# A delta-rule attention and two expert layers on one core: copies moved to DMA, squares to ScalarE, and a shorter inversion of the first four tiles

## Chip, cores and metric

The kernel runs on one core of one Trainium2 chip. The metric is the device time of one execution, in microseconds (us). Lower is better. The kernel before takes 950.15 us (median of 3 runs, 949.26 to 957.06).

## What is computed

An attention with a delta-rule state feeds a mixture-of-experts layer, and that feeds a second one. The change touches the attention alone:

```python
k_n = k / (np.linalg.norm(k, axis=-1, keepdims=True) + 1e-06)
for t in range(S):                      # B=4, H=8, S=768, D=48
    y[:, :, t] = einsum('bhd,bhde->bhe', q[:, :, t], state)
    v_old = einsum('bhde,bhd->bhe', state, k_n[:, :, t])
    state += beta[:, :, t] * outer(k_n[:, :, t], v[:, :, t] - v_old)
x = y as rows of tokens (3072 x 384)
x = moe(x, ...)     # each token to the expert with the largest logit
x = moe2(x, ...)    # each expert takes N/E tokens, largest logits first
```

## The kernel before

**Tiles.** The tokens are 24 tiles of 128, six to a batch. A tile holds 8 heads and two chunks of 64 tokens, so 16 blocks of 64x64. Inside a chunk the recurrence over tokens becomes a triangular solve: with A the strictly triangular matrix of products of keys, scaled by beta, the inverse of I + A is applied to keys and values (`solve`), and only then does the state pass from chunk to chunk (`chain`).

**One tile's preparation.** `a_trans` (L202) transposes keys and queries on TensorE (PE), `a_copy` (L216) brings them to the tile KQ on ScalarE (ACT), `a_gram` (L224) multiplies them, and `a_mask` (L234) scales by beta and masks, into the tile AT. The mask is done on VectorE (DVE) by line L243, or split: ACT scales (L241) and GpSimd (POOL) multiplies with the mask (L247). `a_diag` (L249) copies the 32x32 blocks on the diagonal to Dc, on ACT (L263), POOL (L261) or DVE (L259), as the tables `DP` and `DIA` say. `kbeta` (L196) and `vscale` (L189) are multiplications on POOL. Norms: `norm_sq` squares keys (L156 on POOL, but L153 and L154 on DVE and ACT for the first four tiles), `norm_sum` and `norm_fin` add and invert on DVE, with a root on ACT between them (L168).

**The inversion.** `stage_b` (L265) inverts the 32x32 blocks of four tiles at once on DVE: a transposition (L269), 30 steps of a multiplication (L280) and an addition (L284), and two transpositions out (L288, L290). It is a generator: `bs(k)` takes k pieces of it. Group 0 (tiles 0 to 3) is inverted before the loop starts, group g during the four tiles before its use; the tables `NB0`, `NB1`, `MB` and `PB` say how many pieces go where. `place` (L293) copies the inverted blocks into XT, half on ACT (L300) and half on POOL (L298), and `join1`, `join2` (L303, L317) make the off-diagonal 32x32 block of each 64x64 inverse by small matmuls on PE (L312, L324) with copies on ACT (L315, L327).

**The loop.** `go` (L406) first prepares eight tiles, then runs over n = 0 to 24. Iteration n does `solve(n)` (L339: 8 matmuls with 128x128 weights), `zcopy` on ACT (L343), `prod` (L353), `psub` on DVE (L357), then `chain(n)` in two halves (L379), while it prepares tile n+8, pieces of a stage are taken on DVE, and XT is filled for tile n+1. There is one XT, so `place(n+1)` comes after `solve(n)`. Each engine takes its instructions in the written order. The SyncE queue (SP) issues nearly all DMAs: the token loads of `load_tok` (two per tile), `store` of a tile (L399) and, in iterations 2, 5, 8 and 11, sixteen loads of keys and values for three tiles (L138).

**After the loop** the expert layers run; the change leaves them as they are.

```python
            if n % 4 == 0 and g < NG:          # L513, in the loop
                self.b = self.stage_b(g)
            bs(nb)
            if 0 < n < NT:
                for c in range(2):
                    self.solve(n, c)
                    self.zcopy(c)
```

Of the kernel before, what the change touches and what calls it, by code (L numbers as in the profile page):

```python
# [28 lines left out]
WM = (30, 2, 3)  # L29
HB = 60  # L30
# [5 lines left out]
class Attention:  # L36
    def __init__(self, tc, ctx, q, k, v, beta, w_gate, bias_t, consts, xbuf, LG):
# [14 lines left out]
        self.KQ = c1.tile([128, SLOTS, 4, 2, 128], F32, name="KQ")  # L52
# [10 lines left out]
        self.Dc, self.XTc, self.XN, self.R = {}, {}, {}, {}  # L63
# [8 lines left out]
        early = [self.w.tile([128, 32, 32], F32, name=x, bufs=1).rearrange("p u i -> p (u i)").rearrange("p (a h d) -> p a h d", a=2, h=8)  # L72
                 for x in ("XTc", "XN")]
# [72 lines left out]
    def norm_sq(self, n, cnt=3):  # L146
# [102 lines left out]
    def a_diag(self, n, pool=True):  # L249
# [4 lines left out]
        for qd in range(4):  # L254
# [10 lines left out]
    def stage_b(self, g):  # L265
# [5 lines left out]
        yield  # L271
        nc.vector.memset(X.rearrange("p i j -> p (i j)")[:, 0:1024:33], 1.0)
        for j in range(1, 31):
            m = 31 - j

            h = (17 if j < 11 else 24 if j < 19 else 28 if j < 25 else 30) - j - 1
            parts = [(0, h), (h, m)] if g == 0 and min(h, m - h) * j >= HB else [(0, m)]
            t = tmp[:, :m * j].rearrange("p (i c) -> p i c", c=j)
            for i, k in parts:
                nc.vector.tensor_mul(t[:, i:k], X[:, j + 1 + i:j + 1 + k, j:j + 1].to_broadcast([128, k - i, j]),  # L280
                                     X[:, j:j + 1, :j].to_broadcast([128, k - i, j]))
            yield
# [1553 lines left out]
```

## Time and profile before

| what | value |
| --- | --- |
| median of 3 runs | 950.15 us (949.26 to 957.06) |
| the profiled execution | 951.86 us |
| its span, first to last instruction | 950.1 us |
| mean granted TensorE clock | 0.944 of 2.4 GHz |
| PE, weight loads, DVE, ACT, POOL busy | 834.7, 746.8, 657.3, 454.1, 335.5 us |

The profile is one execution recorded by the hardware. Times in it count from its first instruction; 1.76 us of the execution lie outside of the span. A row of a timeline has the start, the duration, the engine, the line, what is written and read, the shapes, the number of merged instructions, and in brackets the idle time of the engine ahead of it with what ended it. A row of windows has the stretch, its length, the busy time of each engine with the number of instructions, the granted TensorE clock, the DMA share and GB/s.

### The profile page before, as it was taken

How to read it: one execution, taken by the hardware profiler on the slowest of the kernel's cores; microseconds unless marked ns; L12 is line 12 of the kernel's file. 1: busy time of each engine (PE TensorE's matmuls, PEld its weight loads, DVE VectorE, ACT ScalarE, POOL GpSimd, SP SyncE). 2: the span in 40 equal slices, each digit the busy share in tenths (PEclk: the TensorE clock that was granted, in tenths of full speed). 3: DMA queues.
4: the chain of work that ended last, by engine and by line, in shares of the span. 5: the costliest groups of instructions: out<-in, count | busy, mean ns of one | idle time of the engine just before them, and what ended most of it. 6: DMA issues, size and time to landing. Idle time of an engine off the chain costs nothing. (4 is left out here: it accounts for less than half of the span.)

```text
span 950.1 us, 22994 instructions
## 1 busy us (share of the span) xinstructions
PE 834.7 (88%) x9024; PEld 746.8 (79%) x9031; DVE 657.3 (69%) x1744; ACT 454.1 (48%) x990; POOL 335.5 (35%) x504
## 2 busy tenths in 40 slices
PE   5559879897888996999999999988899999897996
PEld 4458768786777885699989999864778888796996
DVE  4997989989797966665744555226877867776531
ACT  3556676585757676445445544220343243233431
POOL 7255444444443122521132221122353444343411
PEclk9877897897979799999999999999999999999999
DMA  9661152342500004563185431402244235324600
GB/s 155 112 107 27 37 101 56 81 80 57 111 11 19 28 28 161 169 221 126 37 284 172 152 107 35 154 29 83 78 170 165 80 123 176 119 66 167 201 26 29
DMA packets 141319, 98.28 MB, mean 103 GB/s; under 512 B 102757, under 2 KB 123268, under 8 KB 141204
## 3 DMA queue, kind: packets, MB, share of 16 engines
q1 hardware_dynamic: 134484, 76.67, 30.0%
q0 software_dynamic: 6720, 20.07, 6.7%
q8 instruction: 74, 1.21, 0.5%
q14 instruction: 41, 0.34, 0.1%
HBM read 82.36 MB, written 14.55 MB: 102 GB/s over the span
## 5 line engine op out<-in xcount | busy, mean ns | idle before, releaser
L1079 PE MATMUL ph<-xT,HL 128*128 128x384 f32 x1152 | 232.4, 345 | 11.2 <-DVE hh L1087 9.4
L1099 PE MATMUL po<-HL,hh 128*128 128x384 f32 x1152 | 238.3, 345 | 0.2 <-DVE hh L1087 0.2
L1079 PEld LDWEIGHTS ph<-xT,HL 128*128 128x128 f32 x1152 | 202.2, 190 | 21.4 <-DVE hh L1087 11.7
L1099 PEld LDWEIGHTS po<-HL,hh 128*128 128x128 f32 x1152 | 196.9, 189 | 3.6 <-issue 0.7
L1082 ACT ACTIVATE hh<-ph 128x384 fp32r<-128x384 f32 x128 | 62.7, 491 | 180.1 <-PE ph L1079 167.2
L1050 DVE TENSOR_TENSOR HL<-raw,HL 128x768 fp32r<-128x768 f32 x104 | 105.4, 1023 | 57.8 <-ACT HL L1049 57.4
L1087 DVE SCALAR_TENSOR_TENSOR hh<-ph,hh 128x384 fp32r<-128x384 f32 x128 | 70.6, 552 | 80.2 <-ACT hh L1082 80.1
L1049 ACT ACTIVATE HL<-raw 128x768 fp32r<-128x768 f32 x128 | 103.4, 839 | 33.7 <-DMA raw<-in_moe_w_dram 33.7
L280 DVE TENSOR_TENSOR Dtmp<-Dt 128x30 f32<-128x30 f32 (+22 forms) x199 | 89.2, 456 | 3.9
L379 PE MATMUL pc<-SI,R 112*48 112x56 f32 (+1 forms) x1536 | 65.2, 239 | 20.8 <-DVE R L357 16.5
L284 DVE TENSOR_TENSOR Dt<-Dt,Dtmp 128x30 f32<-128x30 f32 (+22 forms) x199 | 80.4, 412 | 3.0
L379 PEld LDWEIGHTS pc<-SI,R 112*48 112x48 f32 (+1 forms) x1536 | 57.4, 148 | 28.9 <-DVE R L357 19.8
L357 DVE TENSOR_TENSOR R<-pz,C 112x448 f32<-112x448 f32 x96 | 57.2, 614 | 19.5 <-ACT lgr L387 10.8
L1050 POOL TENSOR_TENSOR HL<-raw,HL 128x768 fp32r<-128x768 f32 x24 | 46.4, 1942 | 64.3 <-ACT HL L1049 64.2
L1137 POOL DMA_INDIRECT x2buf<-x,pidx x24 | 23.8, 990 | 106.1 <-ACT x L1133 86.1
L339 PE MATMUL pz<-RK,XT 128*128 128x96 f32 x384 | 60.4, 323 | 0.0
L353 PE MATMUL pz<-AT,Z 64*112 64x112 f32 x768 | 52.6, 279 | 7.4 <-ACT Z L343 7.3
L232 PE MATMUL pa<-KQ 64*64 64x128 f32 x640 | 49.0, 302 | 10.3 <-ACT KQ L221 10.2
L339 PEld LDWEIGHTS pz<-RK,XT 128*128 128x128 f32 x384 | 56.1, 232 | 1.6
L353 PEld LDWEIGHTS pz<-AT,Z 64*112 64x112 f32 x768 | 44.0, 184 | 12.5 <-ACT Z L343 9.2
L232 PEld LDWEIGHTS pa<-KQ 64*64 64x64 f32 x640 | 40.0, 150 | 14.1 <-ACT KQ L221 11.3
L1605 POOL DMA_INDIRECT out_dram<-x,oid x24 | 25.6, 1066 | 55.9 <-ACT x L1602 46.1
(408 smaller groups left out, 1257.3 us busy)
## 6 DMA issues: line engine op xcount, KB each, us to landing
raw<-in_moe_w_dram SPq DMA_DIRECT2D x68, 768.0 KB, 6.8
xbuf<-xt SPq DMA_DIRECT2D x24, 196.0 KB, 2.0
qt<-in_q_dram SPq DMA_DIRECT2D x22, 192.0 KB, 3.9
kt<-in_k_dram SPq DMA_DIRECT2D x21, 192.0 KB, 3.6
RK<-in_k_dram SPq DMA_DIRECT2D x48, 72.0 KB, 2.8
RK<-in_v_dram SPq DMA_DIRECT2D x48, 72.0 KB, 2.7
RK<-in_k_dram SPq DMA_DIRECT2D x8, 96.0 KB, 4.5
RK<-in_v_dram SPq DMA_DIRECT2D x8, 96.0 KB, 3.1
```

The lines of the kernel that those rows point to most:

```text
L232: nc.tensor.matmul(pg[r, p], KQ[:, 0:64], KQ, start=True, stop=True)
L280: nc.vector.tensor_mul(t[:, i:k], X[:, j + 1 + i:j + 1 + k, j:j + 1].to_broadcast([128, k - i, j]), X[:, j:j + 1, :j].to_broadcast([128, k ...
L284: nc.vector.tensor_add(X[:, j + 1 + i:j + 1 + k, :j], X[:, j + 1 + i:j + 1 + k, :j], t[:, i:k])
L339: nc.tensor.matmul(pz[:, p], self.XT[0][:, u], self.RK[:, n % RSLOTS, u], start=True, stop=True)
L353: nc.tensor.matmul(self.pr[h][:, p], self.Z[r, u], self.AT[r, n % SLOTS, u, 64:176], start=True, stop=True)
L379: nc.tensor.matmul(self.pc[r, hd], self.Rb[n % 2][0:112, hd % 2, c, hd // 2, r], SI[0:112, hd], start=True, stop=True)
L1049: nc.scalar.activation(t[:, i, 0, c], self.raw[s][i][:, c], AF.Copy)
L1050: (nc.gpsimd if pool else nc.vector).tensor_sub(t[:, i, 1, c], self.raw[s][i][:, c], t[:, i, 0, c].bitcast(F32))
L1079: nc.tensor.matmul(self.ph, W[:, i, a, c], x[:, k, b], start=(k == 0 and n == 0), stop=(k == 2 and n == 2))
L1082: nc.scalar.activation(h[:, 0], self.ph, AF.Relu)
L1087: self.nc.vector.scalar_tensor_tensor(h[:, 1], ph, 0.0, h[:, 0].bitcast(F32), op0=OP.max, op1=OP.subtract)
L1099: nc.tensor.matmul(self.po[s][t], h[:, a, r], W[:, 2 + i, b, c], start=(f == 0 and n == 0), stop=(f == 7 and n == 2))
```

## The change

Five things are changed, all in the attention.

1. Squares of keys (`norm_sq`) go from POOL to ACT for all tiles after the first four.
2. In the loop, `a_diag` of three tiles in four goes from POOL to four DMAs on SP (table value 3), and `place` of tiles 2 to 23 goes from ACT and POOL to four DMAs on SP.
3. `solve` takes each 128x128 matmul as two of 64x64, on the halves of the partitions.
4. For group 0, `stage_b` is rewritten: it inverts 16x16 blocks (14 steps, both blocks of a 32x32 block in one instruction). `join0a` and `join0b` then make the 32x32 inverses of one tile: 32 and 48 matmuls of 32x32, one subtraction and three scaled additions on DVE. The old way is kept as `stage_c` for the groups 1 to 5. Both inverses now lie in one tile, XTN, with two buffers.
5. The preparation is reordered: `go` writes out the first tiles, tiles 4 to 7 are masked whole on DVE, `stage_b(0)` runs in one piece before their masks, and the products, masks and diagonals of tiles 6 and 7 go into iterations 0 and 1. `stage_c(1)` starts in iteration 1 (before: 0) and is paced by new tables NF0, NF1. The idle matmuls of `warm` are no longer called. KQ keeps two slots of keys and eight of queries.

```diff
-NB0, NB1 = (7, 8, 8, 30), (3, 6, 0, 3)
+NB0, NB1, NF0, NF1 = (7, 8, 8, 30), (3, 6, 0, 3), (0, 12, 12, 30), (0, 8, 6, 0)
-SPL, DIA, QO = (0, 0, 1, 0), (0, 1, 1, 1), (0, 1, 1, 1)
+SPL, DIA, QO = (0, 0, 1, 0), (0, 3, 3, 3), (0, 1, 1, 1)
...
 def norm_sq
-            nc.gpsimd.tensor_mul(sq, K, K)
+            nc.scalar.activation(sq, K, AF.Square)
...
 def a_diag
+            elif pool == 3:
+                nc.sync.dma_start(o, i)
...
 def stage_b
+        def blocks(i, j, rows, cols):
+            x = X[:, i:i + 1, j:j + 1]
+            n, m = rows[0], cols[0]
+            return bass.AP(tensor=x.tensor, offset=x.offset, ap=[x.ap[0], [528, 2], [rows[1], n], [cols[1], m]])
+        nc.vector.memset(X[:, 16:32, 0:16], 0.0)
+        nc.vector.memset(X.rearrange("p i j -> p (i j)")[:, 0:1024:33], 1.0)
+        for j in range(1, 15):
+            m = 15 - j
+            t = tmp[:, :2 * m * j].rearrange("p (b i c) -> p b i c", b=2, c=j)
+            nc.vector.tensor_mul(t, blocks(j + 1, j, (m, 32), (j, 0)), blocks(j, 0, (m, 0), (j, 1)))
+            yield
+            r = blocks(j + 1, 0, (m, 32), (j, 1))
+            nc.vector.tensor_add(r, r, t)
+            yield
+        yield from self.turn(g, X)
...
+    def join0a(self, n):
...
+        for u in range(8):
+            for qd in range(4):
+                r, i0 = slice(32 * qd, 32 * qd + 32), 32 * (qd % 2)
+                nc.tensor.matmul(pt[r, u], self.AT[r, sl, u, i0:i0 + 32], D[r, u], start=True, stop=True)
+        nc.vector.tensor_sub(t0, pt, D)
+    def join0b(self, n):
...
+        for u in range(8):
+            for qd in range(4):
+                r = slice(32 * qd, 32 * qd + 32)
+                nc.tensor.matmul(px[r, 0, u], t0[r, u], DT[r, u], start=True, stop=True)
+        for u in range(8):
+            for qd in (0, 2):
+                r = slice(32 * qd, 32 * qd + 32)
+                nc.tensor.matmul(px[r, 1, u], DT[r, u], t0[r, u], start=True, stop=True)
+        for qd in (0, 2):
+            r = slice(32 * qd, 32 * qd + 32)
+            nc.vector.scalar_tensor_tensor(D[r], D[r], 2.0, px[r, 1], op0=OP.mult, op1=OP.add)
+        nc.vector.scalar_tensor_tensor(DT, DT, 2.0, px[:, 0], op0=OP.mult, op1=OP.add)
...
 def place
-            if qd % 2:
-                self.nc.gpsimd.tensor_copy(self.XT[0][r, :, r], self.XTc[n // 4][r, us])
+            if n > 1:
+                self.nc.sync.dma_start(self.XT[0][r, :, r], self.of(n, 0)[r])
...
 def solve
-            nc.tensor.matmul(pz[:, p], self.XT[0][:, u], self.RK[:, n % RSLOTS, u], start=True, stop=True)
+            for h in range(2):
+                r = slice(64 * h, 64 * h + 64)
+                nc.tensor.matmul(pz[r, p], self.XT[0][r, u, r], self.RK[r, n % RSLOTS, u], start=True, stop=True)
...
 def go
+        self.join0a(0)
+        self.join0b(0)
+        self.norm_sum(6, 3)
+        self.norm_root()
+        self.place(0)
+        self.vscale(0, 1)
+        self.join1(0)
+        self.join0a(1)
+        masks(4)
+        self.join2(0)
+        self.join0b(1)
+        self.vscale(1, 3)
+        masks(5)
+        self.norm_fin(6, 3)
...
             if n == 0:
                 for c in range(2):
                     self.solve(n, c)
                     self.zcopy(c)
+                self.join0a(2)
+                gram(6)
+                self.join0b(2)
+                masks(6)
...
```

On DVE, the kernel before has this from the last pieces of group 0's stage to the first of group 1's (L288 and L290 transpose group 0 out, L269 transposes group 1 in, and its steps begin):

```order
L288 STREAM_TRANSPOSE XN<-Dt 128x32x32
L290 STREAM_TRANSPOSE XTc<-Dt 128x32x32
L269 STREAM_TRANSPOSE Dt<-Dc 128x1024
L272 MEMSET Dt 128x32
L280 TENSOR_TENSOR Dtmp<-Dt 128x30
L284 TENSOR_TENSOR Dt<-Dt,Dtmp 128x30
L280 TENSOR_TENSOR Dtmp<-Dt 128x58
L284 TENSOR_TENSOR Dt<-Dt,Dtmp 128x29x2
```

The changed kernel has this ahead of group 1's first transposition (L297), in iterations 0 and 1: L334 is the subtraction of `join0a`, L350 and L351 are the additions of `join0b`, L418 is `psub(0)`, and the masks L243 are those of tile 6, then of half of tile 8 and of tile 7:

```order
L334 TENSOR_TENSOR t_816<-pm,XTN 128x256
L350 SCALAR_TENSOR_TENSOR XTN<-XTN,pm 32x256 x2
L351 SCALAR_TENSOR_TENSOR XTN<-XTN,pm 128x256
L243 SCALAR_TENSOR_TENSOR AT<-pa,bp,mask 128x128 x8
L418 TENSOR_TENSOR R_95<-pz,C_92 112x448 x4
L334 TENSOR_TENSOR t_1049<-pm,XTN 128x256
L350 SCALAR_TENSOR_TENSOR XTN<-XTN,pm 32x256 x2
L351 SCALAR_TENSOR_TENSOR XTN<-XTN,pm 128x256
L243 SCALAR_TENSOR_TENSOR AT<-pa,bp,mask 128x128 x12
L297 STREAM_TRANSPOSE Dt<-Dc 128x1024
```

The joins of tiles 2 and 3, twenty mask instructions and `psub(0)` now stand ahead of that transposition, and the joins of tiles 0 and 1 with the masks of tiles 4 and 5 stand ahead of these.

On SP the kernel before has, from the end of iteration 5 to that of iteration 6 (the sixteen loads, tile 16's tokens, the store of tile 5):

```order
L138 DMA RK<-in_k_dram 64x6x48 x8
L138 DMA RK<-in_v_dram 64x6x48 x8
L127 DMA kt_87<-in_k_dram 128x8x48
L127 DMA qt_89<-in_q_dram 128x8x48
L399 DMA xbuf<-xt 128x392
```

and the changed kernel, in the same place:

```order
L138 DMA RK<-in_k_dram 64x6x48 x8
L138 DMA RK<-in_v_dram 64x6x48 x8
L261 DMA Dc<-AT 32x8x32 x4
L127 DMA kt_87<-in_k_dram 128x8x48
L127 DMA qt_89<-in_q_dram 128x8x48
L357 DMA XT_91<-XTN 32x8x32 x4
L460 DMA xbuf<-xt 128x392
```

The copies of `a_diag` (L261) and of `place` (L357) now stand in SP's order behind the sixteen loads, the second of them ahead of the next tile's `solve`.

On PE, the changed kernel has between the last transposition before the loop and the first `solve` (L400): L333 is `join0a`, L343 and L347 `join0b`, L372 `join1`, L383 `join2`:

```order
L333 MATMUL pm<-XTN,AT 32x32 x32
L343 MATMUL pm<-XTN,t_546 32x32 x32
L347 MATMUL pm<-t_546,XTN 32x32 x16
L372 MATMUL pm<-XTN,AT 32x32 x16
L333 MATMUL pm<-XTN,AT 32x32 x32
L383 MATMUL pm<-XTN,t_641 32x32 x16
L343 MATMUL pm<-XTN,t_661 32x32 x32
L347 MATMUL pm<-t_661,XTN 32x32 x16
L400 MATMUL pz<-RK,XT_91 64x96 x16
```

All of these write the one buffer of `pm`, each after its reader on DVE or ACT is done; before, only `join1`, `join2` and the idle matmuls stood there.

## Rows read from the trace of the kernel before

**Rows 1.** All-engine windows: the inversion of group 0, then iterations 4 to 15.

```profile
31.00:78.00 47.00, 25.49 (x286) 23.33 (x287) 46.03 (x126) 20.75 (x63) 20.47 (x18) 0.75 0.55 98
130.00:297.60 167.60, 144.21 (x2594) 127.88 (x2592) 148.72 (x336) 112.86 (x291) 73.24 (x108) 0.88 0.32 66
```

**Rows 2.** DVE timeline, from the first masks to iteration 9.

```profile
22.36 1.13 DVE L243 SCALAR_TENSOR_TENSOR AT<-pm,bp,mask 128x128 f32<-128x128 f32 x4 [1.21 <-PE pm L232]
...
33.75 2.09 DVE L284 TENSOR_TENSOR Dt<-Dt,Dtmp 128x30 f32<-128x30 f32 x1
...
44.68 1.33 DVE L165 TENSOR_REDUCE nt<-sq 128x24 f32<-128x1152 f32 x1
...
75.29 1.93 DVE L269 STREAM_TRANSPOSE Dt<-Dc 128x1024 f32<-128x1024 f32 x1
...
83.94 0.62 DVE L357 TENSOR_TENSOR R<-pz,C 112x448 f32<-112x448 f32 x1 [4.63 <-PE pz L353]
...
98.54 0.40 DVE L280 TENSOR_TENSOR Dtmp<-Dt 128x228 f32<-128x228 f32 x1
...
150.23 0.47 DVE L280 TENSOR_TENSOR Dtmp<-Dt 128x228 f32<-128x228 f32 x1
...
168.38 1.82 DVE L280 TENSOR_TENSOR Dtmp<-Dt 128x150 f32<-128x150 f32 x1
...
185.04 2.20 DVE L357 TENSOR_TENSOR R<-pz,C 112x448 f32<-112x448 f32 x4
...
204.67 0.61 DVE L357 TENSOR_TENSOR R<-pz,C 112x448 f32<-112x448 f32 x1
```

**Rows 3.** Windows of L280 (two rows), then of L284 (two rows): DVE time.

```profile
130.00:297.60 167.60, 46.74 (x90) 0.88 0.32 66
297.60:339.00 41.40, 9.98 (x30) 0.84 0.05 18
...
130.00:297.60 167.60, 37.47 (x90) 0.88 0.32 66
297.60:339.00 41.40, 10.06 (x30) 0.84 0.05 18
```

**Rows 4.** ACT timeline of the prologue: the first squares, tile 3's copy, tile 0's place.

```profile
10.89 0.84 ACT L154 ACTIVATE sq<-RK 128x768 f32<-128x768 f32 x1 [5.28 <-DMA RK<-in_k_dram]
...
24.31 0.59 ACT L221 ACTIVATE KQ<-pz 128x512 f32<-128x512 f32 x1
...
75.43 0.84 ACT L300 ACTIVATE XT<-XTc 32x256 f32<-32x256 f32 x2
```

**Rows 5.** PE timeline: joins of tiles 0 and 1, solves of tiles 7 and 9, a late join.

```profile
73.55 1.06 PE L312 MATMUL pm<-XN,AT 32*32 32x32 f32 x32 [11.92 <-DVE XN L288]
...
83.77 0.69 PE L312 MATMUL pm<-XN,AT 32*32 32x32 f32 x32
...
170.53 2.02 PE L339 MATMUL pz<-RK,XT 128*128 128x96 f32 x16
...
199.31 2.03 PE L339 MATMUL pz<-RK,XT 128*128 128x96 f32 x16
...
353.31 0.69 PE L324 MATMUL pm<-XTc,t 32*32 32x32 f32 x32 [0.55 <-ACT t L315]
```

**Rows 6.** Windows of L156 (squares), then of L261 (diagonal copies): POOL time.

```profile
130.00:297.60 167.60, 6.32 (x3) 0.88 0.32 66
...
130.00:297.60 167.60, 15.29 (x36) 0.88 0.32 66
```

**Rows 7.** SP timeline of iteration 5: the sixteen loads.

```profile
159.40 6.13 SPq L138 DMA_DIRECT2D RK<-in_k_dram  x8
165.58 5.55 SPq L138 DMA_DIRECT2D RK<-in_v_dram  x8
```

**Rows 8.** DMA issues by line on the page: queue, count, KB each, us to landing.

```profile
xbuf<-xt SPq DMA_DIRECT2D x24, 196.0 KB, 2.0
```

**Rows 9.** DVE waits up to iteration 24: us in total, times, longest.

```profile
DVE Dt L269 <- ACT Dc L263: 13.9, 3, 5.4
```

More of the change, by code (lines that the diff above doesn't have):

```diff
@@ L71, in __init__ @@
             nc.vector.memset(self.qt[i][:, :, 48:], 0.0)
-        early = [self.w.tile([128, 32, 32], F32, name=x, bufs=1).rearrange("p u i -> p (u i)").rearrange("p (a h d) -> p a h d", a=2, h=8)
-                 for x in ("XTc", "XN")]
+        early = self.w.tile([128, 2, 32, 32], F32, name="XTN", bufs=2)
+        early = [early[:, i].rearrange("p u i -> p (u i)").rearrange("p (a h d) -> p a h d", a=2, h=8) for i in range(2)]
         for x in early:
@@ L282, in stage_b @@
             yield
-            for i, k in parts:
-                nc.vector.tensor_add(X[:, j + 1 + i:j + 1 + k, :j], X[:, j + 1 + i:j + 1 + k, :j], t[:, i:k])
+            nc.vector.tensor_add(X[:, j + 1:, :j], X[:, j + 1:, :j], t)
             yield
-        xt = self.XTc[g] = w.tile([128, 32, 32], F32, name="XTc", bufs=1)
-        xn = self.XN[g] = w.tile([128, 32, 32], F32, name="XN", bufs=1)
-        nc.vector.transpose(xn.rearrange("p u j -> p j u"), X.rearrange("p i j -> p j i"))
+        yield from self.turn(g, X)
@@ L323, in join2 @@
                 a, m = slice(64 * h, 64 * h + 32), slice(64 * h + 32, 64 * h + 64)
-                nc.tensor.matmul(px[a, u], self.t1[m, u], self.XTc[n // 4][m, u0 + u], start=True, stop=True)
+                nc.tensor.matmul(px[a, u], self.t1[m, u], self.of(n, 0)[m, u], start=True, stop=True)
         for h in range(2):
@@ L414, in norm, with gram, masks @@
             self.norm_fin(n, cnt)
+        def gram(n):
+            for c in range(2):
+                self.a_gram(n, c)
+        def masks(n):
+            self.kbeta(n)
+            for c in range(2):
+                self.a_mask(n, c)
         self.norm_sq(0, 4)
-        self.warm(WP[0])
         self.a_trans(0, "pz", 4)
-        self.warm(WP[1])
         self.a_copy(0)
@@ L426, in go @@
         self.a_copy(1)
-        for c in range(2):
-            self.a_gram(0, c)
-        self.warm(WP[2])
+        gram(0)
         self.norm_fin(0, 4)
@@ L477, in go @@
-        next(side, None)
-        self.vscale(0, 4)
-        self.a_diag(7, DP[7])
-        bs(99)
-        self.warm(WM[0], "pz", 4)
+        gram(1)
+        self.load_k(6, 3, sync)
+        self.load_v(0, 4, sync)
+        self.a_trans(3, "pz", 4)
+        self.a_copy(3)
+        next(side, None)
+        self.late_init(w_gate)
+        self.norm_sq(4, 2)
+        masks(0)
+        self.norm_sum(4, 2)
+        self.norm_root()
+        self.a_diag(0, DP[0])
+        gram(2)
+        masks(1)
@@ new lines, in go @@
+        self.a_diag(1, DP[1])
+        gram(3)
+        self.a_trans(4, "pz", 4)
+        masks(2)
+        self.a_diag(2, DP[2])
+        self.a_copy(4)
+        gram(4)
+        self.a_trans(5, "pz", 4)
+        masks(3)
+        self.a_diag(3, DP[3])
+        self.b = self.stage_b(0)
+        bs(99)
+        self.a_copy(5)
+        self.a_trans(6, "pz", 4)
+        gram(5)
+        self.a_copy(6)
+        self.a_trans(7, "pz", 4)
+        self.norm_fin(4, 2)
+        self.norm_sq(6, 3)
+        self.a_copy(7)
@@ L509, in go @@
                 self.qcopy(n)
+            if n == 1:
+                gram(7)
+                masks(7)
+                self.a_diag(6)
+                self.a_diag(7, False)
+                self.b = self.stage_c(g)
+                bs(1)
             if Dn and m - 1 < NT:
@@ L553, in go @@
                 self.a_gram(m, 1)
+            if n == 0:
+                self.join0a(3)
             if n > 18:
```

126 lines of the change are left out of this document (52 added, 74 removed).

## Prediction, before the changed kernel was run

> **What bounds the kernel now.** Read the windows over all engines first [rows 1]. From 31 to 78 us, while the first four tiles are inverted, DVE is busy for 46.03 of 47 us and PE for 25.49. Over the iterations 4 to 15 DVE is busy for 148.72 of 167.6 us; PE's 144.21 comes close, but holds waits for DVE's results in pipelined form. So up to about 300 us the end of each tile is set by DVE, in its written order, and what a change does is read there. Next comes the DVE timeline [rows 2]: an addition of 30 elements takes 2.09 us at 33.75, and a multiplication of 150 takes 1.82 at 168.38, where one of 228 takes 0.40 at 98.54. Such stretched operations stand beside work on POOL. The windows of the two step lines tell how much that is [rows 3]: iterations 16 to 19, where POOL has hardly any work, spend 9.98 + 10.06 = 20.0 us on a group's sixty steps, and the three groups before them 46.74 + 37.47 = 84.2 us, 24.1 more than three times 20.0. After 372 us the expert layers run, which the change leaves alone; I count them at nothing.
>
> **The start: group 0 and tiles 4 to 7.** Old stage 0 runs on DVE from 33.75 to group 1's transposition at 75.29 [rows 2], 41.5 us; less its two transpositions out at 1.93, 37.6. The norms of tiles 4 to 8 lie between its pieces and stay: a reduction of 1.33 [rows 2] and sixteen small operations, together about 4.5 by my estimate at 0.2 each. The new stage has 28 steps of 28 to 112 elements; sixty undisturbed steps of larger sizes take 0.33 on average [rows 3], and I take 0.28, so 7.8, and 0.4 for two memsets. That is 24.9 less. DVE gains masks of four tiles, which ACT and POOL made before: four masks take 1.13 [rows 2], eight per tile, 9.0 in all. It also gains four joins of four operations of 256 elements, about 0.4 each between the 0.28 of a mask and the 0.62 of a `psub` of 448 [rows 2]: 6.4. DVE's work falls by 9.5 us. In iterations 0 to 3, POOL's two squares and most copies go too, some 4 us by the prices below. DVE's old wait of 4.63 at 83.94 for the first product [rows 2] goes, replaced by what follows.
>
> Then the new waits. The reduction of tiles 4 and 5 now stands ahead of tile 1's masks, behind squares on ACT that stand behind tile 3's copy. That copy ends at 24.31 + 0.59, the squares need 0.84 [rows 4], the reduction about 0.9, so tile 1's masks start near 26.7 instead of 22.36 [rows 2]: 4.3 later.
>
> The joins are a string PE, DVE, PE, DVE, ACT on one PSUM buffer. Sixteen matmuls of 32x32 (the trace records each twice) took 1.06 us for tile 0 and 0.69 for tile 1 [rows 5], 66 and 43 ns each; so `join0a` is 1.4 to 2.1 us, `join0b` 2.1 to 3.2. DVE's waits by that: 3.4 for tile 0's `join0b`; 7.0 for tile 1, where the root, `place` with 0.84 on ACT [rows 4], `join1` and `join2` come between; 3.8 for tile 2; 3.5 for the first product, whose transposes wait for tile 6's masks to free their buffers; 5.9 for tile 3; 3.1 for tile 7's products and its diagonal on ACT. The sum is 26.7 with the slower rate in the prologue, 24 with the faster everywhere, and 19 if four quadrants at work instead of two halve the time per matmul. I take 21, between the last two. The start so costs -9.5 - 4 - 4.6 + 4.3 + 21 = **+7 us**, between +5 and +13. The loop itself starts earlier, its first `solve` about ten us; but group 1's stage starts some twenty later, and it decides.
>
> **The steady loop, iterations 4 to 15.** POOL loses three squares, 6.32 us, 36 diagonal copies, 15.29 us [rows 6], and 24 `place` copies of the same size. A square costs DVE about 1.5: 1.82 against at most 0.4 [rows 2]; three are 4.5. A copy costs little: at 150.23, in the middle of four of them, 228 elements take 0.47 instead of 0.40 [rows 2], so 15% of the time, 2.3 us for the diagonals and 1.5 for the rest. Relief: 8.3 us.
>
> The Trainium skill, "SBUF — State Buffer", section "SBUF: two separate sides", says that GpSimd and a DVE operation with two SBUF inputs lock a shared port pair in turn, and the later one blocks for the whole instruction. For squares and masks the rows agree; for one-input copies they don't, since 0.47 is far from 0.40 plus a copy's 0.42. By the rule the copies would have held DVE for up to 25 us, and with the squares that is more than the whole excess of 24.1, in which POOL's masks and scalings have their share; the sum goes by the rows.
>
> Against it stands SP. In iteration 5 sixteen loads occupy SP from 159.40 to 171.1 [rows 7]. Behind them now stand four diagonal DMAs, two token loads and the four `place` DMAs of tile 7, without which `solve(7)` can't run. The small DMAs lie between 0.34 and the 0.77 of a load (6.13 for 8); I take 0.5, and a landing of 2.0 [rows 8]: 171.1 + 2 + 1.1 + 2 + 2 = 178.2. Before, `solve(7)` ran at 170.53 [rows 5]. But `psub(7)` was at 185.04 [rows 2], and from solve to `psub` it takes 5.4, as tile 9 shows (199.31 to 204.67) [rows 2, 5]: 183.6 is still in time. So the lateness is covered by DVE's own lag, with 1.4 to spare. DVE can't become faster there than that, though: the same holds for tile 10. Of the relief about half of what falls in these stretches (4.8 us) is lost, 2.4, and I add 1 for the queue. ACT gets squares of some 1.2 us, waiting in order for loads of keys, as POOL did; DVE's lag covers it, and without that cover it would be some 3 us per square. DVE's waits for ACT's diagonal copies, 13.9 in three [rows 9], shrink by `place`'s 0.84 each; I take 2. Sum: -8.3 + 2.4 + 1 - 2 = **-6.9 us**, between -11 and +10.
>
> **The tail.** In the last four tiles, without a stage, `join2` waits 0.55 for ACT's copy of `join1` [rows 5], which stood behind `place`; it goes: **-2.2 us**, between 0 and -4. `solve` by halves has twice the matmuls with a quarter of the weights each; 2.02 us per tile [rows 5] may become anything from 1.0 to 4.0, hidden behind DVE up to tile 19 and priced in the range for the last four; I take no change.
>
> **The sum.** 7 - 6.9 - 2.2 = -2.1 on the profiled execution's 951.86, so 949.8; that execution is 1.7 above the median of the runs shown, so **948 us** is what I expect of a median.
>
> **Rivals.**
> - *The joins are cheap and SP is in time.* If masks and quadrants fill the waits, DVE waits 12 instead of 21, the full 8.3 counts, the squares' place on ACT is free, and the tail gives 3: 951.9 - 2 - 8.3 - 2.5 - 3 - 1.7 = 934. For it: DVE's work alone falls by 9.5 at the start. Against: one PSUM buffer carries all joins. The Trainium skill, "TensorEngine Tiling (Array Packing)", section "Key Properties", has different tiles load and multiply in parallel, which speaks for this rival; no row here shows four at work. Chance 0.27.
> - *One-input copies block DVE fully.* Then the 24.1 us of excess holds up to 12 us more that leaves with the copies, as against my 3.8: 938 with some of it lost to SP. For it: DVE operations of 0.9 or so do occur beside POOL. Against: 0.47 at 150.23. It is the lock rule named above. Chance 0.07.
> - *The queue behind the loads decides.* If the small DMAs take 0.77 each, `place` of tile 7 lands near 180.4; with PE at 1.2 GHz after the wait (1.06 against 0.69 for the same matmuls [rows 5]) the way to `psub` is 9 instead of 5.4: 189.4 against 185.04. That is 4.4 for tile 7 and for tile 10, 2 for tile 13, and the relief falls to 3.5; the joins at the slower rate cost 12. 951.9 + 12 - 3.5 + 10.8 - 2 - 2.2 - 1.7 = 965. It decides from a landing later than 179.6, 1.4 after mine. For it: SP's order, shown above. Against: an undisturbed store is issued in 0.34. Chance 0.21.
>
> The forecast itself has 0.45; its own range is 940 to 958. About 1%, or 9.5 us, is what a measurement of this kernel can tell from no change: faster means under 940.6, slower over 959.7. Faster: 0.24 of the first rival, 0.06 of the second, 0.03 of the forecast, 0.33 in all. Slower: 0.20 of the third and 0.02 of the forecast, 0.22. The rest, 0.45, lies within. The range of 8 in 10 reaches from a little beyond the first rival to just short of the third, 930 to 963.
>
> **What would show it.** In the changed profile the first `solve` should start near 68 us, group 1's first transposition near 90 to 98, and DVE's waits for PE between the two stages should add up to about 21. Groups of steps should cost 2 to 3 us less each than the 28 of before. `place` of tiles 7 and 10 should land some 19 us after the loads began, with `psub` of these tiles waiting little. The forecast is wrong if group 1's stage starts by 85, or if DVE waits for those products by several us.

## The result: 961.28 us, slower by 1.1%, and the profile after

| | us, median (runs) | ratio [95% interval] |
| --- | --- | --- |
| before | 950.43 (949.26 to 957.06, 4) | |
| changed | 961.28 (960.05 to 964.55, 4) | 1.0108 [1.0081, 1.0135] |

The forecast was 948, range 930 to 963. The time lies in the range and on the wrong side of no change. The profiled execution is the slowest of the four, 964.55 with a span of 962.8, so it stands 12.7 behind the profiled one of before (950.1).

**The start.** DVE timeline of the changed kernel, with DVE's waits in brackets (L350: `join0b`, L334: `join0a`, L418: `psub`, L297: group 1's first transposition):

```profile
52.97 0.84 DVE L350 SCALAR_TENSOR_TENSOR XTN<-XTN,pm 32x256 f32<-32x256 f32 x2 [2.02 <-PE pm L347]
...
58.47 0.42 DVE L334 TENSOR_TENSOR t<-pm,XTN 128x256 f32<-128x256 f32 x1 [2.96 <-PE pm L333]
...
62.83 0.84 DVE L350 SCALAR_TENSOR_TENSOR XTN<-XTN,pm 32x256 f32<-32x256 f32 x2 [1.88 <-PE pm L347]
...
71.38 0.84 DVE L350 SCALAR_TENSOR_TENSOR XTN<-XTN,pm 32x256 f32<-32x256 f32 x2 [1.34 <-PE pm L347]
...
78.25 1.16 DVE L418 TENSOR_TENSOR R<-pz,C 112x448 f32<-112x448 f32 x2 [3.53 <-PE pz L414]
80.91 1.16 DVE L418 TENSOR_TENSOR R<-pz,C 112x448 f32<-112x448 f32 x2 [1.50 <-PE pz L414]
85.38 0.42 DVE L334 TENSOR_TENSOR t<-pm,XTN 128x256 f32<-128x256 f32 x1 [3.31 <-PE pm L333]
87.63 0.84 DVE L350 SCALAR_TENSOR_TENSOR XTN<-XTN,pm 32x256 f32<-32x256 f32 x2 [1.82 <-PE pm L347]
...
94.09 1.91 DVE L297 STREAM_TRANSPOSE Dt<-Dc 128x1024 f32<-128x1024 f32 x1 [1.83 <-ACT Dc L265]
...
133.60 2.18 DVE L418 TENSOR_TENSOR R<-pz,C 112x448 f32<-112x448 f32 x4
```

The bracketed waits add up to 20.2 us. The last row is `psub(3)`; before it ran at 125.44, so up to tile 3 the change costs 8.2 us.

**The loop.** SP timeline of iteration 5, which answers to [rows 7], and what is now behind the loads:

```profile
167.62 5.53 SPq L138 DMA_DIRECT2D RK<-in_k_dram  x8
173.19 6.18 SPq L138 DMA_DIRECT2D RK<-in_v_dram  x8
179.47 2.60 SPq L261 DMA_DIRECT2D Dc<-AT  x4
182.17 0.55 SPq L127 DMA_DIRECT2D kt<-in_k_dram  x1
182.82 0.53 SPq L127 DMA_DIRECT2D qt<-in_q_dram  x1
183.40 2.86 SPq L357 DMA_DIRECT2D XT<-XTN  x4
```

`place(7)` is issued 15.8 us after the loads began. PE timeline: the solves of tiles 7, 8 and 10 (to be held against [rows 5]):

```profile
187.20 3.33 PE L400 MATMUL pz<-RK,XT 64*64 64x96 f32 x32 [7.24 <-DMA XT<-XTN]
199.75 1.54 PE L400 MATMUL pz<-RK,XT 64*64 64x96 f32 x32
...
232.12 3.25 PE L400 MATMUL pz<-RK,XT 64*64 64x96 f32 x32 [11.20 <-DMA XT<-XTN]
```

PE waits for `place`, and the solve behind such a wait takes twice as long. Of tile 10 the loads begin at 211.56, so its solve starts 20.6 us after them. DVE then waits for the products of these tiles:

```profile
194.51 1.15 DVE L418 TENSOR_TENSOR R<-pz,C 112x448 f32<-112x448 f32 x2 [3.78 <-PE pz L414]
...
239.19 0.62 DVE L418 TENSOR_TENSOR R<-pz,C 112x448 f32<-112x448 f32 x1 [4.05 <-PE pz L414]
```

PE's waits for `place` over the whole span (us in total, times, longest):

```profile
PE pz L400 <- DMA XT<-XTN: 32.7, 7, 11.2
```

DVE's waits between `psub(3)` and `psub(15)`, in the kernel before and then in the changed one (for products, for ACT's diagonal copies, and for the root of the norms on ACT):

```profile
DVE Dt L269 <- ACT Dc L263: 8.6, 2, 5.4
DVE nt L176 <- ACT nt L168: 4.3, 4, 3.4
DVE R L357 <- PE pz L353: 0.9, 2, 0.5
...
DVE R L418 <- PE pz L414: 11.0, 7, 4.1
DVE Dt L297 <- ACT Dc L265: 9.7, 2, 5.3
DVE nt L176 <- ACT nt L168: 7.2, 4, 3.4
```

The steps of three groups, windows of L304 and L306 over tiles 4 to 15, from `solve(4)` to `solve(16)`:

```profile
144.96:307.95 162.99, 39.63 (x88) 0.87 0.43 81
...
144.96:307.95 162.99, 35.19 (x89) 0.87 0.43 81
```

They sum to 74.8 us for 177 steps, against 84.2 for 180 in [rows 3]: the steps did become cheaper, by some 3 us a group. What DVE saved, it waited: 14.1 us more than before, 10.1 of them for products.

### The profile page after: what moved, and what is told of

Same layout as the page of the kernel before. It is cut to its first block, busy times and chain, and to the rows that moved or that the text cites. A ratio compares the mean times of both kernels' runs of the same rounds, so it can differ in the third digit from the quotient of the medians.

```text
span 962.8 us, 24907 instructions
## 1 busy us (share of the span) xinstructions
PE 828.7 (86%) x9985; PEld 737.4 (77%) x9985; DVE 634.6 (66%) x1723; ACT 432.3 (45%) x909; POOL 276.1 (29%) x410
## 5 line engine op out<-in xcount | busy, mean ns | idle before, releaser
L1164 PEld LDWEIGHTS ph<-xT,HL 128*128 128x128 f32 x1152 | 203.2, 191 | 22.2 <-DVE hh L1172 11.2
L1167 ACT ACTIVATE hh<-ph 128x384 fp32r<-128x384 f32 x128 | 62.7, 491 | 185.8 <-PE ph L1164 159.3
L400 PE MATMUL pz<-RK,XT 64*64 64x96 f32 x768 | 52.5, 293 | 34.9 <-DMA XT<-XTN 32.7
L418 DVE TENSOR_TENSOR R<-pz,C 112x448 f32<-112x448 f32 x96 | 57.2, 617 | 31.0 <-PE pz L414 23.6
L400 PEld LDWEIGHTS pz<-RK,XT 64*64 64x64 f32 x768 | 45.6, 167 | 38.3 <-issue 31.2
L440 PEld LDWEIGHTS pc<-SI,R 112*48 112x48 f32 (+1 forms) x1536 | 56.5, 146 | 20.3 <-DVE R L418 10.1
L304 DVE TENSOR_TENSOR Dtmp<-Dt 128x30 f32<-128x30 f32 (+9 forms) x150 | 61.2, 408 | 3.4
L306 DVE TENSOR_TENSOR Dt<-Dt,Dtmp 128x30 f32<-128x30 f32 (+9 forms) x150 | 59.6, 397 | 3.0
L459 POOL COPY xt<-LG 128x8 f32<-128x8 f32 x24 | 4.9, 204 | 195.5 <-DVE LG L456 79.8
L414 PEld LDWEIGHTS pz<-AT,Z 64*112 64x112 f32 x768 | 45.0, 187 | 11.6 <-ACT Z L404 6.9
```

The lines of the kernel that those rows point to most:

```text
L304: nc.vector.tensor_mul(t, X[:, j + 1:, j:j + 1].to_broadcast([128, m, j]), X[:, j:j + 1, :j].to_broadcast([128, m, j]))
L306: nc.vector.tensor_add(X[:, j + 1:, :j], X[:, j + 1:, :j], t)
L400: nc.tensor.matmul(pz[r, p], self.XT[0][r, u, r], self.RK[r, n % RSLOTS, u], start=True, stop=True)
L414: nc.tensor.matmul(self.pr[h][:, p], self.Z[r, u], self.AT[r, n % SLOTS, u, 64:176], start=True, stop=True)
L440: nc.tensor.matmul(self.pc[r, hd], self.Rb[n % 2][0:112, hd % 2, c, hd // 2, r], SI[0:112, hd], start=True, stop=True)
L1164: nc.tensor.matmul(self.ph, W[:, i, a, c], x[:, k, b], start=(k == 0 and n == 0), stop=(k == 2 and n == 2))
```

## The experiments

One table for all. The lag is the start of the first `psub` of a tile less that of the kernel before (from the DVE timelines; before: 125.44, 185.04, 225.45, 293.04, 367.71 for tiles 3, 7, 10, 15 and 23); the last column is the difference of the spans. Each ratio is taken against runs of the kernel before made beside that kernel, whose median lay between 950.4 and 953.2 us; so compare ratios rather than times. Lags and spans come from one execution each, and the kernel before itself ran from 946.4 to 958.0 us, so a difference of 1 or 2 us between two lags is not clear of scatter.

| kernel | us | ratio [interval] | 3 | 7 | 10 | 15 | 23 | span |
| --- | --- | --- | --- | --- | --- | --- | --- | --- |
| changed | 961.28 | 1.0108 [1.0081, 1.0135] | 8.2 | 9.5 | 13.7 | 10.0 | 9.5 | 12.7 |
| e1_place_copies | 951.92 | 1.0011 [0.9991, 1.0030] | 7.3 | 4.7 | 1.7 | -2.8 | -0.7 | 0.1 |
| e2_v_after_place | 955.35 | 1.0046 [1.0019, 1.0072] | 6.8 | 3.6 | 1.8 | 1.2 | 0.9 | 2.0 |
| e4_prologue_part | 963.49 | 1.0114 [1.0084, 1.0144] | 9.1 | 8.5 | 9.3 | 9.5 | 13.9 | 14.6 |
| e5_place_actq | 964.88 | 1.0153 [1.0111, 1.0196] | 4.9 | 3.5 | 5.1 | 3.6 | 10.2 | 12.4 |
| e7_e1_full | 952.87 | 1.0030 [1.0003, 1.0057] | 5.8 | 4.5 | 1.2 | -2.2 | -2.1 | 0.5 |
| e8_joins_early | 944.61 | 0.9904 [0.9869, 0.9939] | -2.1 | -4.6 | -7.1 | -11.4 | -7.3 | -5.7 |
| e9_old_stage | 947.93 | 0.9945 [0.9919, 0.9970] | 2.1 | -0.4 | -2.3 | -6.7 | -4.9 | -2.9 |
| e10_joins_diag | 943.68 | 0.9899 [0.9868, 0.9929] | -1.9 | -3.9 | -6.6 | -11.6 | -11.1 | -8.9 |
| b1_loop_parts | 950.21 | 0.9984 [0.9969, 0.9999] | -3.7 | -0.7 | 2.5 | -1.1 | -2.6 | -2.0 |
| b2_no_place | 938.34 | 0.9869 [0.9828, 0.9910] | -3.0 | -3.8 | -5.5 | -10.1 | -9.3 | -12.9 |
| b3_squares | 946.35 | 0.9950 [0.9927, 0.9973] | -1.7 | -3.5 | -4.0 | -6.1 | -5.6 | -5.5 |
| b4_diag | 951.59 | 1.0015 [0.9991, 1.0039] | -2.1 | -3.6 | -2.0 | -2.5 | 0.0 | -1.2 |
| b6_place | 952.25 | 0.9995 [0.9962, 1.0028] | -0.8 | 0.3 | 3.1 | 0.7 | 0.2 | 0.3 |
| b7_full_solve | 941.57 | 0.9870 [0.9810, 0.9931] | -2.8 | -4.5 | -6.9 | -11.2 | -8.3 | -9.3 |
| b8_diag_dve | 937.53 | 0.9836 [0.9801, 0.9870] | -4.0 | -6.0 | -9.0 | -14.1 | -13.8 | -13.8 |

Kernels e are the changed kernel with an edit, kernels b the kernel before with one.

### Is it place on SP?

**e1_place_copies**: `place` as copies again.

```diff
-            if n > 1:
-                self.nc.sync.dma_start(self.XT[0][r, :, r], self.of(n, 0)[r])
-            elif qd % 2:
+            if qd % 2:
```

> The changed kernel, with place of all tiles on ACT and POOL again (copies instead of four DMAs on SP). Theory Q (the DMAs of place behind the sixteen loads on SP delay the solves of tiles 4, 7, 10 and 13, and this eats what the loop gains): the start still costs its 8 us, the loop gains some 8 to 11, so 950 us (947 to 953), and no solve waits for a DMA for over 1 us, against 7.5, 7.2, 11.2 and 4.1 now. Rival S (the solves would be as late without the DMAs, since ACT's and PE's chain at the lower clock is late by itself, and the whole loss is the start's): 959 to 962, with the waits moved to copies on ACT or to PE.

Measured 951.92. The same start (7.3), but from tile 3 to tile 15 it gains 10.1 us where the changed kernel loses 1.8. PE timeline of this run, the solves of tiles 7 and 10:

```profile
176.06 1.90 PE L398 MATMUL pz<-RK,XT 64*64 64x96 f32 x32
...
213.28 1.90 PE L398 MATMUL pz<-RK,XT 64*64 64x96 f32 x32
```

No wait stands before them. Theory Q of the expectation holds, its rival S falls.

**e2_v_after_place**: the loads of values go behind `place`.

```diff
                 self.place(n + 1)
+                if n % 3 == 0 and 0 < n and n + 9 < NT:
+                    self.load_v(n + 9, 3, [self.nc.sync])
...
                 self.load_k(n + 10, 3, [self.nc.sync])
-                self.load_v(n + 10, 3, [self.nc.sync])
```

> The changed kernel, with the eight loads of values moved on SP from the end of iterations 2, 5, 8, 11 to behind place in the next iteration, so that only the eight loads of keys stand ahead of place. Theory Q: place of tiles 4, 7, 10, 13 is issued some 5.5 to 6 us earlier, DVE's waits for the products of tiles 7 and 10 (3.8 and 4.1) go, and the time falls to 954 us (951 to 957). Rival S: it changes nothing, 960 to 962; if the values come too late for their scaling, it is slower than that.

Measured 955.35: two thirds of the loss are gone with half of the loads ahead. So it is the order on SP that counts, by its length.

**e5_place_actq**: the same DMAs from ACT's queue.

```diff
-                self.nc.sync.dma_start(self.XT[0][r, :, r], self.of(n, 0)[r])
+                self.nc.scalar.dma_start(self.XT[0][r, :, r], self.of(n, 0)[r])
```

> The changed kernel, with the four DMAs of place issued from ACT's queue, where no loads stand ahead of them. If SP's order is the cause of the late solves: 951 us (949 to 954), and place is issued within 1 us of the solve before it or of its stage. If a DMA's own landing of 2.8 us, or the transfer of the loads in the same engines, delays place wherever it is issued: 957 to 961. ACT's own time for four issues would add up to 2 us to either.

Measured 964.88, above both cases of the expectation; but in the place of the loss it was right: no solve waits for a DMA any more, and tile 10 lags no more than tile 3 did (5.1 and 4.9), where the changed kernel added 5.5. But nothing is gained either, and the tail loses 6.6. ACT timeline of this run: four issues, and ACT's next instruction behind them:

```profile
185.91 2.66 ACTq L357 DMA_DIRECT2D XT<-XTN  x4
188.62 0.76 ACT L375 ACTIVATE t<-pm 32x256 f32<-32x256 f32 x2 [3.98 <-DVE bp L183]
```

ACT starts nothing in the 2.66 us of its four issues, where ACT's two copies took 0.84 [rows 4]. That this is what takes the gain, and what the tail loses, was not tested.

**b1_loop_parts** and **b2_no_place**: the kernel before with its own start, and the loop's parts with and without `place`.

```diff
-SPL, DIA, QO = (0, 0, 1, 0), (0, 1, 1, 1), (0, 1, 1, 1)
+SPL, DIA, QO = (0, 0, 1, 0), (0, 3, 3, 3), (0, 1, 1, 1)
...
-            nc.gpsimd.tensor_mul(sq, K, K)
+            nc.scalar.activation(sq, K, AF.Square)
```

Both have this and solve by halves; b1 also has `place` by DMA:

```diff
+            if n > 1:
+                self.nc.sync.dma_start(self.XT[0][r, :, r], self.XTc[n // 4][r, us])
```

> The kernel before with its own start, and with the loop's parts of the change alone (place and diagonals as DMAs on SP, squares on ACT, solve by halves). Theory Q: what POOL no longer does to DVE and what the queue costs cancel: 951 us (948 to 954), with solves of tiles 7 and 10 waiting for place. As I forecast the loop (-6.9 and -2.2 in the tail): 941. Rival S has no loss in the loop either: 941 to 945.

> The kernel before with its own start, diagonals as DMAs on SP, squares on ACT and solve by halves, but place as copies on ACT and POOL. By the terms of the prediction (squares -4.5, diagonals -2.3, nothing lost on SP): 943 us. By the run of the changed kernel with place copied, which made good some 8 us between its fourth tile and its end: 939 to 941. If the gain there came from slack that the longer start had built up, and not from POOL: 947 to 950.

Measured 950.21, as theory Q had it, and 938.34, 0.7 under the second case. On the old start too, `place` on SP takes back what the other parts give: from tile 3 to 15, b2 gains 7.1 us and b1 loses 2.6, a difference of 9.7; on the new start it was 11.9.

**b6_place**: that last edit alone on the kernel before.

> The kernel before with place of the tiles 2 to 23 as DMAs on SP alone. With the diagonals and squares off POOL this part cost 11.9 us (950.2 against 938.3). If its cost is the queue behind the loads alone, less what DVE's lag covers (larger here, since POOL's squares still stretch DVE's work): 954 to 960. If it costs only together with the diagonals' DMAs, which stand ahead of it on SP and take 2.6 us: 949 to 952.

Measured 952.25, no difference, and for a reason that the expectation had only in part. PE timeline (tiles 7 and 10), then DVE timeline of the same tiles:

```profile
177.04 3.70 PE L341 MATMUL pz<-RK,XT 128*128 128x96 f32 x16 [6.87 <-DMA XT<-XTc]
...
219.62 3.70 PE L341 MATMUL pz<-RK,XT 128*128 128x96 f32 x16 [7.44 <-DMA XT<-XTc]
...
185.29 1.16 DVE L359 TENSOR_TENSOR R<-pz,C 112x448 f32<-112x448 f32 x2 [0.77 <-PE pz L355]
...
228.51 0.62 DVE L359 TENSOR_TENSOR R<-pz,C 112x448 f32<-112x448 f32 x1
```

PE waits 7 us for `place` here too, the solves are 6.5 and 10.0 late (before: 170.53 and 209.67), and DVE waits 0.77 and nothing. From `psub(3)` to `psub(15)` DVE waits 4.0 us for products in this kernel, 9.8 in b1 and 0.9 before. With DVE as slow as before, its lag covers most of the queue: tile 10 is 3.1 late, tile 15 only 0.7. With DVE faster (b1), the same queue decides.

### What did POOL's work cost DVE?

**b3_squares** has the squares' line of the diff of b1 and b2 alone, **b4_diag** the diagonals' alone, **b7_full_solve** both without the halves.

> The kernel before with the squares of the tiles from 4 on on ACT alone. By the prediction's price of about 1.5 us per square for three squares in iterations 4 to 15, and as many for the two squares in iterations 0 to 3 and the one beside the start's stage: -7 to -9, so 942 to 944 us. If ACT's wait for the keys or DVE's waits for ACT's copies take that back: 947 to 950.

> The kernel before with the diagonals of three tiles in four as DMAs on SP alone. By the prediction's price of a one-input copy on POOL (15% of its time, 2.3 us in all, with nothing else on the path): 948 us (947 to 949). If such a copy holds DVE for its whole time, as the second rival had it: 940 or less. If the wait of the DMAs for the masks delays the token loads and the stores behind them on SP: 951 to 955.

> The kernel before with diagonals on SP and squares on ACT, and solve as before (the kernel of 938.3 us without the halves). The parts alone gave -4.7 (squares) and +0.5 (diagonals), together with the halves -12.8. If the halves carry what is missing: 946 us. If the two copies' work on POOL was hiding the one behind the other, or stretches of low clock fell otherwise: 938 to 942.

Measured 946.35, 951.59 and 941.57: the squares lie between their two cases, the diagonals in their last, the pair without the halves in its last. Windows of the two step lines over tiles 4 to 15, as in [rows 3]. Squares alone:

```profile
128.30:291.50 163.20, 44.76 (x90) 0.90 0.33 67
...
128.30:291.50 163.20, 36.51 (x90) 0.90 0.33 67
```

Diagonals alone:

```profile
127.90:295.10 167.20, 46.80 (x90) 0.87 0.37 74
...
127.90:295.10 167.20, 38.39 (x90) 0.87 0.37 74
```

Both with the halves (b2):

```profile
129.00:287.50 158.50, 41.63 (x90) 0.91 0.40 77
...
129.00:287.50 158.50, 34.73 (x90) 0.91 0.40 77
```

The stretch was 167.6 before. Squares off POOL: 163.2, so -4.4, and steps of 81.3 for 84.2. Diagonals off POOL: 167.2, and steps of 85.2, so nothing. Together 158.5 and 76.4: twice the sum of the parts. b7 shows that it is the pair and not the halves (159.25 and 79.1 in its windows; the lag falls by 8.4 from tile 3 to 15 there, by 7.1 in b2; the ratios are 0.9870 and 0.9869).

The traces tell in part why the copies count only once the squares are gone. As an estimate, take of each step the time above the shortest step of its form in the same run, and put it down to the POOL instruction that the step overlaps longest. Before, that is 26.6 of the 84.2 us: 11.2 beside POOL's masks (L247), 5.2 beside `vscale` (L194), 3.4 beside squares, 2.5 beside `kbeta` (L198), 2.7 beside the 36 diagonal copies and 1.0 beside those of `place`. In b4 the 2.7 are gone, but squares (4.7) and `kbeta` (4.2) take 3.0 back: without copies ahead of them POOL reaches them earlier, beside other steps. From b3 to b7 the copies' share, 2.4 there, goes too, and `kbeta` takes 0.8 back. DVE's waits for ACT's diagonal copies do the rest: they rise from 8.6 to 9.9 us in b4, and fall from 9.7 to 7.5 between b3 and b7; why was not settled.

**e4_prologue_part**: the new start, with the loop's copies and squares as before (`place` as in e1, `DIA` at 1, squares of tiles 9 on on POOL).

> The changed kernel, with the loop's copies and squares as they were before (place on ACT and POOL, diagonals and the squares of tiles 9 on on POOL); the new start, the joins and solve by halves stay. If the start's loss of 8 us is carried to the end: 958 us (956 to 961). If DVE's slack later in the loop takes it up (the tiles of the tail are not bound by DVE's order): 950 to 953.

Measured 963.49, above both cases. The start's 9.1 us are carried from tile 3 to tile 15 without change (9.5); nothing in the loop takes them up. At tiles 16 and 20 it loses 2.2 more each, which the expectation had not; more on tile 20 follows below.

**e7_e1_full**: e1 with solve as eight matmuls again.

> The changed kernel with place copied, and with solve as eight matmuls of 128x128 weights again. If the halves are worth nothing, as forecast: 950 to 954 us. If sixteen matmuls in halves are faster by the half microsecond per tile that the trace shows (1.54 against 2.03) and it counts in the last four tiles only: 953 to 955; if it counts in the loop too: 960.

Measured 952.87 against e1's 951.92, with overlapping intervals: the halves are worth nothing that can be measured, though a solve takes 1.54 us for 2.03 where the granted clock is 1.00.

### What is the new start worth?

**e8_joins_early**: e1 with the joins two by two ahead of the loop, in buffers of their own.

```diff
-        pt = self.ps.tile([128, 8, 32], F32, name="pm", bufs=1)
-        self.t0 = t0 = self.w.tile([128, 8, 32], F32, name="t0", bufs=1)
+        pt = self.ps.tile([128, 8, 32], F32, name="pz", bufs=4)
+        t0 = self.w.tile([128, 8, 32], F32, name="t0", bufs=2)
...
-        px = self.ps.tile([128, 2, 8, 32], F32, name="pm", bufs=1)
+        px = self.ps.tile([128, 2, 8, 32], F32, name=("pm", "pc")[n % 2], bufs=1)
...
         self.join0a(0)
+        self.join0a(1)
         self.join0b(0)
...
+        masks(5)
+        self.join0a(2)
+        self.join0a(3)
+        self.join2(0)
+        masks(4)
+        self.join0b(2)
```

**e9_old_stage**: e1 with `stage_c(0)` in place of `stage_b(0)`, which gives the inverses of 32x32 blocks at once, and so without `join0a` and `join0b`.

> The changed kernel with place copied (as in the run of that name, 951.9 us), and with the joins of the four tiles written two by two, each with PSUM buffers and a copy of its own, ahead of the loop and among the masks of tiles 4 and 5, so that DVE has work while PE joins. If the joins' waits (13.3 us of DVE time: 2.02, 2.96, 1.88, 1.34, 3.31, 1.82) are what the start loses: the fourth product's subtraction comes some 9 to 12 us earlier than in that run, and the time is 940 to 943 us. If PE is late there by its own matmuls at the lower clock, whatever the order: 949 to 952.

> The changed kernel with place copied, and group 0 inverted by the old sixty steps (32x32 blocks), without the joins of 16x16 blocks; the new order of the start stays. By the prediction's terms the new stage saves 24.9 us and its joins cost 6.4 of work and some 13 of waits, so 951.9 + 24.9 - 19.4 = 957. If sixty steps with POOL silent take the undisturbed 20.0 us, the new stage saves only 12 where the new order has already taken POOL's work away, and the joins cost more than that: 944 us.

Measured 944.61 and 947.93: e8 is 1.6 us above its first case, e9 between its two and nearer the second. DVE's waits in e8 for the joins, from 45 to 100 us:

```profile
DVE XTN L351 <- PE pm L348: 3.5, 2, 1.8
...
DVE t L335 <- PE pz L334: 1.0, 1, 1.0
```

That is 4.5 for the 13.3 of the changed kernel, and tile 3 comes 9.4 us earlier than in e1: the joins' waits were the start's loss. DVE timeline of e9, the first and the last of the sixty steps:

```profile
36.49 0.17 DVE L304 TENSOR_TENSOR Dtmp<-Dt 128x30 f32<-128x30 f32 x1
...
58.20 0.19 DVE L306 TENSOR_TENSOR Dt<-Dt,Dtmp 128x30 f32<-128x30 f32 x1
```

In the new order the old stage takes 21.9 us, near the 20.0 of [rows 3]; POOL has no instruction beside it. The new one takes 8.1 there, so it saves 13.8, and tile 3 comes 5.2 later with it: its joins, as the change has them, cost 19.0 by that difference.

**b8_diag_dve** and **e10_joins_diag**: b2 and e8 with the diagonals of each group's last tile on DVE (`DIA` from `(0, 3, 3, 3)` to `(2, 3, 3, 3)`).

> The kernel of 938.3 us (the kernel before with diagonals on SP, squares on ACT, solve by halves), with the diagonals of each group's last tile copied by DVE instead of ACT. DVE waits for that ACT copy 14 us there, in two groups; four copies of its own are about 1.2 us per group. If the wait is ACT's place in its order: 930 to 934 us. If the mask or the copy ahead of it is what is late: 937 to 940.

> The kernel of 944.6 us (the changed kernel with place copied and the joins ahead of the loop), with each group's last diagonals copied by DVE. The same step took 0.8 us from the kernel of 938.3 in time, and 4.5 at its last product: 940 to 944 us. If it comes below 937.5, the new start beats the old one once its waits are filled; otherwise it doesn't.

Measured 937.53 and 943.68. b8 has the lowest time of all, 0.9836 [0.9801, 0.9870] of before, though its interval overlaps b2's: the old start, with squares on ACT, diagonals on SP and DVE, and `place` as copies. Its lag at tile 23 is 4.5 us less than b2's, its span only 0.9 less, since in b2's profiled execution the expert layers ran 3.6 shorter. The new start, its waits filled, is not better than the old one (e8 against b2, e10 against b8).

## Why the prediction was wrong, step by step

**The start: right in sum.** Forecast +7, measured +8.2. Waits of 21 were forecast and 20.2 are in the rows above; 8.2 for steps and memsets, measured 8.1; group 1's transposition was to come at 90 to 98 and came at 94.09. Some pieces of the list behind the 21 were off both ways, and that they cancel is luck: DVE waits 1.34 for tile 2's `join0b` where the list had 3.8, and 5.03 for the first product where it had 3.5. The first `solve` came at 62.7 instead of near 68. The Trainium skill, "TensorEngine Tiling (Array Packing)", section "Key Properties", has different tiles work in parallel; the trace agrees. PE timeline of the changed kernel, `join0a` on four quadrants and `join1` on two, both at a granted clock of 0.50:

```profile
47.27 1.08 PE L333 MATMUL pm<-XTN,AT 32*32 32x32 f32 x64 [3.46 <-DVE XTN L314]
...
54.39 1.06 PE L372 MATMUL pm<-XTN,AT 32*32 32x32 f32 x32 [1.47 <-DVE XTN L351]
```

Twice the matmuls in the same time. That did not make the joins cheap, as the first rival had it: DVE waits for the string of them, not for their rate.

**The relief: right in sum, not in its parts.** 8.3 for POOL's work and 2 for ACT's were forecast in tiles 4 to 15; e1 gains 10.1 between the lags of tiles 3 and 15, and e4, with POOL's work back in place, loses 0.4. But e1 keeps `place` on ACT and POOL, so only the terms for squares and diagonals (6.8) apply to it; on the old start the same parts gave 7.1 (b2) and 8.4 (b7). ACT's 2 us did not come: DVE's waits for its diagonal copies were 9.7 in the changed kernel and 8.6 before, and those for the root, on which I had put nothing, rose from 4.3 to 7.2. The price of a square held in the loop (-4.5 for three, -4.4 in b3), but the three ahead of it, by the same price another 4.5, gave 1.7 by tile 3. The second rival falls: b4 and b6 each take 36 or 24 of the one-input copies off POOL, and the steps take 85.2 and 84.7 (b6: 47.16 and 37.49 in its windows) for 84.2; by the estimate above the 36 copies, 15.29 us of POOL's time, cost 2.7, where I had 2.3. So for one-input copies the lock rule of the Trainium skill ("SBUF — State Buffer", section "SBUF: two separate sides") has no support here.

**The queue on SP: this step failed.** It read: "So the lateness is covered by DVE's own lag, with 1.4 to spare", and priced what is left at "2.4, and I add 1 for the queue". Measured: 11.9 on the new start, 9.7 on the old one. Of its pieces the landing was nearly right: solve(7) starts 19.6 us after the loads began and solve(10) 20.6, and 18.8 was forecast. Two others were wrong.
- *The way from `solve` to `psub`.* I took 5.4; it was 7.3 for tile 7 (187.20 to 194.51) and 7.1 for tile 10 (232.12 to 239.19). PE had been idle for `place`. Windows of all engines, changed kernel, around `solve(10)`; the granted clock is the first number after POOL's:

```profile
218.00:224.00 6.00, 2.92 (x84) 2.44 (x80) 5.79 (x15) 4.08 (x11) 1.21 (x2) 0.94 0.53 95
224.00:232.10 8.10, 0.00 (x0) 0.01 (x1) 5.82 (x18) 2.50 (x6) 4.54 (x4) 0.50 0.66 104
232.10:236.00 3.90, 3.88 (x47) 3.50 (x48) 2.80 (x8) 0.98 (x2) 0.00 (x0) 0.50 0.35 85
236.00:240.00 4.00, 4.00 (x85) 3.62 (x83) 0.81 (x3) 2.39 (x6) 0.00 (x0) 0.89 0.28 58
```

  PE stands still from 220.9 to 232.1, and in that wait the granted clock falls to 0.50, which is 1.2 of 2.4 GHz. It is still 0.50 in the solve, 3.25 us where `solve(8)` took 1.54 at 1.00, and rises behind it. How much of the loss is this and how much the landing was not separated.
- *The cover itself.* DVE's lag behind PE, 14.5 us at tile 7 before (170.53 to 185.04), is made of the very time that the relief takes away. I saw that ("DVE can't become faster there than that") and charged half of it in two stretches. In b6, with DVE as slow as before, `place` on SP costs 1.5 from tile 3 to tile 15 and 0.3 in the span. Where DVE becomes 7 or 10 us faster (b2, e1), it takes 9.7 or 11.9. The two don't add: the slower of them sets the time, and the queue as it stands allows no gain from DVE.

The third rival named this mechanism, and its price per tile, 4.4, is near DVE's waits of 3.78 and 4.05; it had 0.21. My own sign of being wrong, DVE waiting for those products by several us, is what the profile shows.

Over the profiled execution the forecast's -2.1 and the measured 12.7 are 14.8 apart: 1.2 at the start, 8.7 in the loop (forecast -6.9, measured +1.8), 1.7 in the tail and 3.2 in the expert layers.

**The tail: right but for one tile.** -2.2 was forecast, -0.5 came between tiles 15 and 23. `join2`'s waits for ACT, 1.5 us in three tiles before, are gone, and from tile 20 to 23 the lag falls by 1.6. But tile 20's `psub` lost 2.4 against tile 19's. Windows from the one to the other, in the changed kernel and then in the kernel before:

```profile
344.27:354.63 10.36, 10.03 (x168) 9.00 (x168) 5.20 (x25) 5.27 (x13) 0.84 (x7) 0.58 0.20 45
...
335.53:343.50 7.97, 7.23 (x174) 6.58 (x170) 5.38 (x26) 6.31 (x16) 2.40 (x11) 1.00 0.08 29
```

PE is busy nearly throughout at a granted clock of 0.58, and before it was 1.00. In the other kernels this stretch takes 7.6 to 8.1 us where the clock is 0.99 or 1.00 (b3, b6, e7), 8.7 to 9.3 where it is 0.80 to 0.82 (b1, b2, b8, e1, e9, e10), and 10.0 to 12.0 where it is 0.59 to 0.71 (b4, b7, e4, e5, e8); e2 stands outside, with 10.56 at 0.84. Why the clock is low there in some kernels and not in others stays open.

**The expert layers: counted at nothing.** They took 3.2 us longer in this execution and 3.6 shorter in b2's (span less tile 23's lag), with the same code. The changed kernel's median lies 3.3 under its profiled time, that of before 1.4 under, so some 2 us of the 3.2 may be scatter; b2's median lies 0.6 under, and what gave its gain was not settled.

## What to carry to other kernels

A lag that hides a late transfer and a gain on the engine that lags are the same microseconds: count them once, and ask of every relief what the engine will then wait for. Before small copies go to a DMA queue, read what stands ahead of them there in the iterations with bulk loads, and price a wait of PE with the slower matmuls behind it. A shorter computation that ends in a string of small dependent steps over two engines is worth its time only if other work stands between the steps.

## What the runs showed that I had not expected

- Diagonals off POOL gave nothing alone and some 4 us (163.2 to 159.25 in b7) once the squares were gone as well. Alone, their share of the steps' stretch went over to squares and `kbeta`.
- Most of what POOL costs DVE's steps stands beside its masks and `vscale` (16.4 of 26.6 us), and these the change left on POOL.
- Four DMA issues held ACT for 2.66 us, three times the 0.84 of ACT's two copies, which they replaced together with two of POOL's.
- The same sixty steps took 21.9 us with POOL silent; before, with POOL at work and some norms between, the stage ran for 37.6 by the prediction's count.
- Sixteen matmuls of 64x64 took 1.54 us where eight of 128x128 took 2.03, and 3.33 behind a wait of 7 us.
